# Four edits to an attention, experts and dense-layer kernel: where list scatters and weight loads stand, the mask's number type, and which engines decode w_out

## The chip, the core and the metric

The kernel runs on one core of a Trainium2 chip. A core has a matrix engine (TensorE, PE in the rows, with a separate weight load, PEld), a vector engine (VectorE, DVE), a scalar engine (ScalarE, ACT), a general engine (GpSimd, POOL) and SyncE (SP), which here only starts DMA transfers. The metric is the device time of one execution in microseconds (us), lower is better.

## The reference

Three stages follow one another, cut here to what is computed. The inputs are float32; the dense layer's two matrices arrive as float64.

```python
# attention: q, k, v are (4, 8, 576, 64)
scores = q @ k.T / 8
scores = where(block_of_64(i) >= block_of_64(j), scores, -1e9)
x = softmax(scores) @ v                 # then (2304, 512)
# routed experts: 8 of them, 512 -> 1024 -> 512
do = x @ w_skip > 0
e = argmax(x @ w_gate); gate = softmax(x @ w_gate)[e]
x[do] += gate * (relu(x @ w1[e]) @ w2[e])
# dense layer: 512 -> 2048 -> 512
h = x @ w_in
out = (max(h, 0) + alpha * min(h, 0)) @ w_out
```

## The kernel before

**Attention.** Two heads make a pair, and there are 16 pairs. A hand-written table of times (`OFF`) puts the steps of all pairs in one order. For each pair `sc` makes five tiles of scores. A score is a sum of three matmul groups over a high and a low float32r part of the query and key (`PARTS`); the two heads lie in the two halves of the array's rows. The first four tiles of a pair end with a matmul of `top` by `neg`, in bfloat16, that adds a large negative number to the masked 64 columns (L238). The fifth tile has all 576 columns and no mask (L242).

**Routing.** After each batch (four pairs) the tokens of each expert are ranked. GpSimd scatters each token's number and gate into lists in DRAM (`lst`, L495 in `send`). The rows of x lie in DRAM too (`xd`). For the first 32 rows of each expert there is a shortcut: GpSimd gathers these rows directly (`xgs`), TensorE transposes them, and ScalarE copies the result to `xts` (L687 and L688, in `trans`, called by `s_x`). All other rows are reached through the lists, which SyncE loads back (`load_list`).

**Experts.** `s_one(e)` and `s_two(e)` are the two matmul groups of expert e's first 32 rows. `extra(e)` handles further rows in chunks of up to 128 and is skipped by a branch when there are none; `level0(e)` gathers its first chunk ahead. Expert e+3's weights are loaded during expert e (`load_w`, w1 then w2, 4 pieces of 512 KB each). All large loads stand in one chain in which a load waits for the second-last before it (`DEPTH = 2`, in `bulk`), so two are in flight. `DEC[e]` says how many pieces of w_in or w_out are decoded during expert e before and after that load. A decode turns pairs of integers (a float64) into a float32, and then splits it into a high and a low part; each one also issues the load three pieces on, into one of three raw buffers (`dr`). From `last_exp` on the order is written by hand: routing, experts, then the dense layer.

**Dense layer.** Five windows of 512 rows (the last has 256). For every f of 16, `g1` is the first matmul group, `act` the slope and the split into `gh` (ScalarE) and `gl`, and `g2` the second group. `g1` runs two f ahead of `g2`, `act` one ahead. In the first window (w = 0, called window 0 here) the loop also decodes w_out, f+3 at step f (`w_dec`, with a part on ScalarE and GpSimd: L637, L648, L649) and splits it (`w_split`, L629 for the low part). At odd f it transposes 128 rows of the next window (`tr_x`) and splits them into `xs` (`split_x`, L853 on ScalarE and L854 on VectorE). The first two pieces of w_out are decoded during expert 5 by VectorE alone, into a tile called `xz`; the first window's rows also go to `xz` (L887), are transposed there (L896) and the last experts' results are added by TensorE (L899, which reads a selection matrix that VectorE makes at L882).

## Time and profile before

| | us |
|---|---|
| median of 3 runs | 865.99 (864.88 to 866.8) |
| the profiled execution, its own time | 870.16 |
| the profiled execution, its span | 868.6 |
| TensorE busy in the span | 800.6 (92%) |
| VectorE busy | 459.9 (53%) |
| ScalarE busy | 304.4 (35%) |
| GpSimd busy | 193.7 (22%) |

The profiled execution is one run and took 4.17 us more than the median of the runs. By the rows the span has five stages: attention to about 250 us, the routing tail to 288, the experts to about 406, the last expert with the hand-over to about 443, window 0 to about 542, and the other four windows to the end.

### The profile page before, as it was taken

The page shows a single profiled execution, that of the slowest core. Times are in us where ns is not written, and L with a number is a line of the kernel's source. Part 1 is how long each engine was busy: PE and PEld are TensorE (multiplying, and loading weights), DVE is VectorE, ACT ScalarE, POOL GpSimd, SP SyncE. Part 2 cuts the span into 40 slices and gives each one's busy share as a digit, 9 for nine tenths or more (in the row PEclk, how much of TensorE's full clock was granted, in tenths as well). Part 3 has the DMA queues.
Part 4 walks back from the last instruction along what each step waited for, and adds up shares of the span by engine and source line. Part 5 has one row for each costly group of instructions (what it writes and reads, how often), then busy time and mean ns, then how long its engine had stood idle before and what let it go on. Part 6 is the DMA issues. An engine that isn't in the chain of part 4 may idle for free.

```text
span 868.6 us, 14592 instructions
## 1 busy us (share of the span) xinstructions
PE 800.6 (92%) x5548; PEld 612.0 (70%) x5548; DVE 459.9 (53%) x931; ACT 304.4 (35%) x793; POOL 193.7 (22%) x225
## 2 busy tenths in 40 slices
PE   7999999999985999895499996999999999999998
PEld 4777777777742666663388675888888888888887
DVE  3466758576645397789359998222322222222232
ACT  3667676776631223112143354211121112111121
POOL 1000110100113014223025654222222221222132
PEclk7899999999986999999689999999999999999999
DMA  6674354455315787774632222100020001000000
GB/s 126 149 205 130 93 147 108 116 134 132 88 45 145 241 250 244 248 259 140 213 134 84 74 72 74 48 1 1 1 97 0 1 2 62 11 1 1 25 25 25
DMA packets 96376, 85.80 MB, mean 99 GB/s; under 512 B 68601, under 2 KB 73913, under 8 KB 96272
## 3 DMA queue, kind: packets, MB, share of 16 engines
q1 hardware_dynamic: 93776, 78.88, 31.2%
q0 software_dynamic: 2496, 5.61, 2.1%
q8 instruction: 57, 0.93, 0.4%
q14 instruction: 47, 0.39, 0.1%
HBM read 73.20 MB, written 11.71 MB: 98 GB/s over the span
## 4 chain that ended last, share of the span: by engine, by line
PE 56%; DVE 16%; DMA 15%; issue 5%; ACT 4%; SPq 1%; POOL 1%; another core or an unknown queue 1%; DVEq 0%; ACTq 0%; POOLq 0%
PE psf L966 18%; PE psa L998 6%; PE psa L999 6%; PE psa L1008 6%; DMA w1t<-in_moe_w_dram 5%; DMA w2t<-in_moe_w_dram 5%; PE pso L325 4%; PE pspt L300 4%; PE pss L236 3%; DMA dr<-in_moe_w_in_dram 3%; PE pss L242 2%; PE pso L313 2%; DVE mx L249 2%; DVE dt L638 2%; ACT pt L274 2%
## 5 line engine op out<-in xcount | busy, mean ns | idle before, releaser
L966 PE MATMUL psf<-xs,whi 128*128 128x512 f32 (+1 forms) x640 | 160.7, 373 | 6.1 <-ACT xs L853 6.1
L984 POOL TENSOR_TENSOR gl<-gt,gh 128x512 fp32r<-128x512 f32 (+1 forms) x72 | 85.4, 1186 | 250.5 <-PE psa L1008 136.0
L966 PEld LDWEIGHTS psf<-xs,whi 128*128 128x128 f32 x640 | 115.0, 189 | 31.4 <-ACT xs L853 6.7
L983 ACT ACTIVATE gh<-gt 128x512 fp32r<-128x512 f32 (+1 forms) x80 | 47.1, 588 | 255.7 <-PE psa L999 148.6
L979 DVE TENSOR_SCALAR gu<-psf,alf 128x512 f32<-128x512 f32 (+1 forms) x64 | 43.7, 682 | 165.6 <-PE psf L966 165.3
L966 PE MATMUL psf<-xs,wlo 128*128 128x512 f32 (+1 forms) x320 | 80.9, 375 | 0.0
L266 ACT ACTIVATE pe<-pss,mx 128x512 f32<-128x512 f32 (+3 forms) x128 | 66.6, 525 | 14.5 <-DVE mx L249 12.9
L966 PEld LDWEIGHTS psf<-xs,wlo 128*128 128x128 f32 x320 | 57.2, 189 | 12.0
L274 ACT ACTIVATE pt<-pspt 128x512 f32<-128x512 f32 (+3 forms) x112 | 51.9, 488 | 32.4 <-PE pspt L300 29.6
L998 PE MATMUL psa<-whi,gh 128*128 128x512 f32 x144 | 57.5, 400 | 4.0 <-ACT gh L983 4.0
L249 DVE TENSOR_REDUCE mx<-pss 128x2 f32<-128x1024 f32 (+1 forms) x64 | 52.3, 817 | 14.5 <-PE pss L238 10.5
L998 PE MATMUL psa<-wkg,gh 128*128 128x512 f32 x144 | 56.9, 395 | 2.0 <-ACT gh L983 2.0
L999 PE MATMUL psa<-wlo,gh 128*128 128x512 f32 x144 | 56.3, 391 | 0.0
L999 PE MATMUL psa<-wkg,gh 128*128 128x512 f32 x144 | 56.2, 390 | 0.0
L300 PE MATMUL pspt<-ident,pe 128*128 128x128 f32 x320 | 52.6, 292 | 0.1
L325 PE MATMUL pso<-pt,vr 128*64 128x256 f32 (+1 forms) x384 | 47.1, 356 | 3.6 <-ACT pt L274 3.6
L980 DVE SCALAR_TENSOR_TENSOR gt<-psf,gu 128x512 f32<-128x512 f32 (+1 forms) x64 | 40.0, 625 | 12.3 <-POOL gl L984 6.2
L703 PE MATMUL psh<-w1t,xts 128*32 128x256 f32 x256 | 22.3, 496 | 25.6 <-DMA w1t<-in_moe_w_dram 13.7
L854 DVE TENSOR_TENSOR xs<-psx,xs 128x512 fp32r<-128x512 f32 x18 | 12.4, 689 | 58.1 <-ACT xs L853 58.1
L325 PEld LDWEIGHTS pso<-pt,vr 128*64 128x64 f32 x384 | 29.9, 138 | 17.8 <-ACT pt L274 7.8
L638 DVE TENSOR_SCALAR dt<-dr 128x512 int32<-128x512 int32 x29 | 24.3, 838 | 32.0 <-DMA dr<-in_moe_w_in_dram 27.7
L300 PEld LDWEIGHTS pspt<-ident,pe 128*128 128x128 f32 x320 | 34.6, 144 | 7.1 <-issue 2.2
(237 smaller groups left out, 1455.7 us busy)
## 6 DMA issues: line engine op xcount, KB each, us to landing
w1t<-in_moe_w_dram SPq DMA_DIRECT2D x32, 512.0 KB
w2t<-in_moe_w_dram SPq DMA_DIRECT2D x32, 512.0 KB
dr<-in_moe_w_in_dram SPq DMA_DIRECT2D x16, 512.0 KB
dr<-in_moe_w_out_dram SPq DMA_DIRECT2D x16, 512.0 KB
out_dram<-ob SPq DMA_DIRECT2D x18, 256.0 KB
qr<-in_q_dram SPq DMA_DIRECT2D x32, 128.0 KB
kr<-in_k_dram SPq DMA_DIRECT2D x32, 128.0 KB
vr<-in_v_dram SPq DMA_DIRECT2D x32, 128.0 KB
```

Source lines behind the costliest of these rows:

```text
L249: nc.vector.tensor_reduce(out=m, in_=ps[:, :, 0:128 * i + 128], axis=AX.X, op=ALU.max, negate=True)
L266: ins = nc.scalar.activation(out=pt[:, x, 0:n], in_=ps[:, x, 0:n], func=AF.Exp, bias=m[:, x:x + 1], scale=1.0, accum_out=d["sum"][:, x * 4 ...
L274: nc.scalar.activation(out=o, in_=a, func=AF.Copy)
L300: nc.tensor.transpose(ps[:, y, j, :], e[:, x, j * 128:j * 128 + 128], ident)
L325: nc.tensor.matmul(d["o"][hs, c0:c0 + n * 128], v5[:, j, x, :], pt[:, x, 2 * j:2 * j + n].rearrange("p n c -> p (n c)"), start=(j == 0), s ...
L966: nc.tensor.matmul(ps[:, 0:n], wsp[f // 4 * 4 + kk][a][:, ws], c[:, kk, 0:n], start=(n0 == 0 and kk == 0), stop=(n0 == 2 and kk == 3))
L979: nc.vector.tensor_scalar(out=u[:, 0:n], in0=ps[:, 0:n], scalar1=0.0, scalar2=alf[:, f:f + 1], op0=ALU.min, op1=ALU.mult)
L983: nc.scalar.activation(out=hi[:, 0:n], in_=t[:, 0:n], func=AF.Copy)
L984: (nc.gpsimd if w or f % 2 else nc.vector).tensor_tensor(out=lo[:, 0:n], in0=t[:, 0:n], in1=hi[:, 0:n].bitcast(F32), op=ALU.subtract)
L998: nc.tensor.matmul(o, hi[:, ts], whi, start=(f == 0), stop=False)
L999: nc.tensor.matmul(o, hi[:, ts], wlo, start=False, stop=False)
L1008: nc.tensor.matmul(acc[w, t], lo[:, t * 128:t * 128 + 128], whi, start=False, stop=False)
```

## The change

It has four parts, which the diff shows in the order of the code.

1. The mask's two small operands become float32r, and the mask's matmul stands after the first of the three groups instead of behind the last.
2. The last batch's list scatters are no longer issued in `route5`. They are issued after `s_x(0)`, and the first of them waits for the ScalarE copy of the first rows. Four of the register loads of counts (`load_areg`) stand ahead of it. `s_one` of experts 1 and 2 stand right behind `s_one(0)`.
3. `DEC[4]` becomes (0, 3): during expert 4 the three decodes, with the loads of w_out that they issue, stand behind the load of expert 7's weights.
4. In window 0 the decode of w_out runs on VectorE alone. The negative part is scaled by a second ScalarE operation, the sum is one VectorE operation from PSUM as in the other windows, all `gl` are on GpSimd, and the next window's transposes stand two f earlier, with their split ahead of the decode.

```diff
--- before.py
+++ after.py
@@ -31,7 +31,7 @@
 PADROW = NT
 KX = 4
 DEPTH = 2
-DEC = ((0, 1), (2, 1), (2, 2), (2, 3), (3, 0), (0, 0), (0, 0), (0, 0))
+DEC = ((0, 1), (2, 1), (2, 2), (2, 3), (0, 3), (0, 0), (0, 0), (0, 0))
 ON_ACT = ("0", "1", "2a", "2b", "3a", "3b", "5", "xt")
 PSPLIT = (2, 3)
 EARLY = 2
@@ -144,12 +144,12 @@
     nc.vector.memset(fill, PADROW)
     tlo = acst.tile([128, 5], I32, name="tlo")
     nc.vector.tensor_scalar(out=tlo, in0=tok, scalar1=63, scalar2=None, op0=ALU.bitwise_and)
-    top = acst.tile([128, 128], BF16, name="top")
-    nc.vector.memset(top, 0.0)
+    top = acst.tile([128, 128], F32R, name="top")
+    nc.vector.memset(top.bitcast(F32), 0.0)
     for r in (0, 64):
-        nc.vector.memset(top[r:r + 1, 0:64], 1.0)
-    neg = acst.tile([128, 64], BF16, name="neg")
-    nc.vector.memset(neg, NEG)
+        nc.vector.memset(top[r:r + 1, 0:64].bitcast(F32), 1.0)
+    neg = acst.tile([128, 64], F32R, name="neg")
+    nc.vector.memset(neg.bitcast(F32), NEG)
     thi = acst.tile([128, 5], F32, name="thi")
     nc.vector.tensor_tensor(out=thi, in0=tok, in1=tlo, op=ALU.subtract)
     sli = const.tile([128, 2, 2], F32, name="sli")
@@ -233,9 +233,10 @@
             qc = slice(i * 128, i * 128 + 128)
             for k, (a, b) in enumerate(PARTS):
                 for x, hs in enumerate(half):
-                    nc.tensor.matmul(ps[:, x, 0:n], d[a][hs, qc], d[b][hs, 0:n], start=(k == 0), stop=False)
-            for x, hs in enumerate(half):
-                nc.tensor.matmul(ps[:, x, n - 64:n], top[hs], neg[hs], start=False, stop=True)
+                    nc.tensor.matmul(ps[:, x, 0:n], d[a][hs, qc], d[b][hs, 0:n], start=(k == 0), stop=(k == 2))
+                if k == 0:
+                    for x, hs in enumerate(half):
+                        nc.tensor.matmul(ps[:, x, n - 64:n], top[hs], neg[hs], start=False, stop=False)
         else:
             for c, o in ((slice(0, 512), ps[:, 0]), (slice(512, S), ps[:, 1, 0:64])):
                 for k, (a, b) in enumerate(PARTS):
@@ -490,16 +491,14 @@
         nc.vector.tensor_tensor(out=pi, in0=po, in1=nb, op=ALU.add)
         def send(ts=range(5)):
             for t in ts:
-                if b == B - 1:
+                if t and b == B - 1:
                     apart()
                 ins = nc.gpsimd.indirect_dma_start(out=lst, out_offset=bass.IndirectOffsetOnAxis(ap=pi[:, t, :], axis=0), in_=pr[:, t, :], in_offset=None, bounds_check=LROWS - 1, oob_is_err=False)
                 free(ins, "lst")
-                if b < B - 1:
+                if b < B - 1 or t == 0:
                     tc.add_manual_dep(ins.ins, last_exp[0].name, mybir.DependencyInfo(mybir.DependencyClass.Sync, mybir.DependencyReason.DATA), reason="list scatters apart")
 
         sends[b] = send
-        if b == B - 1:
-            send()
         tg = T5("tg", 3, BF16)
         nc.vector.tensor_copy(out=tg[:, :, 0:1], in_=gate)
         for i in (1, 2):
@@ -665,6 +664,7 @@
                 dec_load(m + 3)
 
     lv = lst.rearrange("(e r) c -> e r c", e=E)
+    AHEAD = 3
     li = [mw.tile([128, E, 2], I32, tag=f"li{i}", name="li", bufs=1) for i in range(KX)]
 
     def load_list(i):
@@ -685,7 +685,7 @@
             ps = ps_t.tile([128, 2, n], F32, tag="t", name="pst", padded_shape=[128, 4, 128])
             for i in range(2):
                 nc.tensor.transpose(ps[:, i], src[0:n, (j + i) * 128:(j + i) * 128 + 128], ident[0:n, 0:n])
-            nc.scalar.activation(out=o[:, j:j + 2, 0:n], in_=ps, func=AF.Copy)
+            last_exp[0] = nc.scalar.activation(out=o[:, j:j + 2, 0:n], in_=ps, func=AF.Copy).ins
 
     sx, sy, sh = {}, {}, {}
 
@@ -701,7 +701,7 @@
         for kk in range(4):
             for c in range(4):
                 nc.tensor.matmul(ps[c * 32:c * 32 + 32, :], sx[g][:, kk, r * 32:r * 32 + 32], wt[e][0][:, kk, c * 256:c * 256 + 256], start=(kk == 0), stop=(kk == 3), tile_position=(0, c * 32))
-        sh[e] = mw.tile([128, 256], F32, tag="sh", name="sh", bufs=1)
+        sh[e] = mw.tile([128, 256], F32, tag="sh", name="sh", bufs=AHEAD)
         nc.scalar.activation(out=sh[e], in_=ps, func=AF.Relu)
 
     def s_ht(e):
@@ -821,6 +821,9 @@
         with many.Else():
             ch.half()
 
+    load_areg(4)
+    s_x(0)
+    sends[B - 1]()
     for i in range(KX):
         load_list(i)
     load_w(2, range(4, 8))
@@ -833,11 +836,11 @@
 
     level0(0)
     level0(1)
-    load_areg(4)
-    s_x(0)
-    tc.mark_branch_hint_location("x0", "LikelyTaken", [ET.PE])
     s_one(0, load_areg)
     load_areg(2)
+    tc.mark_branch_hint_location("x0", "LikelyTaken", [ET.PE])
+    for e in range(1, AHEAD):
+        s_one(e)
     s_ht(0)
     xs = {}
     wkg = []
@@ -862,7 +865,7 @@
             hi, lo = (wk.tile([128, 512], F32R, tag=t, name="w" + t) for t in ("hi", "lo"))
         else:
             return
-        splits[f] = decode(16 + f, hi, lo, tmp, early, False)
+        splits[f] = decode(16 + f, hi, lo, tmp, True, False)
         if not early and f + 3 < 16:
             dec_load(16 + f + 3)
 
@@ -909,7 +912,8 @@
             level0(e + 2)
         if e + 1 < E:
             tc.mark_branch_hint_location(f"x{e + 1}", "LikelyTaken", [ET.PE])
-            s_one(e + 1)
+            if e + 1 >= AHEAD:
+                s_one(e + 1)
         if e + 1 == E:
             first_window()
         else:
@@ -973,15 +977,14 @@
         t = gp.tile([128, 512], F32, tag="gt", name="gt", bufs=1)
         if w == 0:
             nc.scalar.activation(out=u[:, 0:n], in_=ps[:, 0:n], func=AF.Relu, scale=-1.0)
-            nc.scalar.activation(out=t[:, 0:n], in_=ps[:, 0:n], func=AF.Relu)
-            nc.vector.scalar_tensor_tensor(out=t[:, 0:n], in0=u[:, 0:n], scalar=nalf[:, f:f + 1], in1=t[:, 0:n], op0=ALU.mult, op1=ALU.add)
+            nc.scalar.activation(out=u[:, 0:n], in_=u[:, 0:n], func=AF.Copy, scale=nalf[:, f:f + 1])
         else:
             nc.vector.tensor_scalar(out=u[:, 0:n], in0=ps[:, 0:n], scalar1=0.0, scalar2=alf[:, f:f + 1], op0=ALU.min, op1=ALU.mult)
-            nc.vector.scalar_tensor_tensor(out=t[:, 0:n], in0=ps[:, 0:n], scalar=0.0, in1=u[:, 0:n], op0=ALU.max, op1=ALU.add)
+        nc.vector.scalar_tensor_tensor(out=t[:, 0:n], in0=ps[:, 0:n], scalar=0.0, in1=u[:, 0:n], op0=ALU.max, op1=ALU.add)
         hi = gp.tile([128, 512], F32R, tag="gh", name="gh")
         lo = gp.tile([128, 512], F32R, tag="gl", name="gl")
         nc.scalar.activation(out=hi[:, 0:n], in_=t[:, 0:n], func=AF.Copy)
-        (nc.gpsimd if w or f % 2 else nc.vector).tensor_tensor(out=lo[:, 0:n], in0=t[:, 0:n], in1=hi[:, 0:n].bitcast(F32), op=ALU.subtract)
+        nc.gpsimd.tensor_tensor(out=lo[:, 0:n], in0=t[:, 0:n], in1=hi[:, 0:n].bitcast(F32), op=ALU.subtract)
         gt[w, f] = hi, lo
 
     acc = {}
@@ -1018,18 +1021,18 @@
     for n, (w, f) in enumerate(seq):
         if n + 2 < len(seq):
             g1(*seq[n + 2])
-        t = (f - 7) // 2
+        t = (f - 5) // 2
         px = None
         if w + 1 < len(wins) and f % 2 and 0 <= t < wins[w + 1][1] // 128:
             px = tr_x(w + 1, t)
         if n + 1 < len(seq):
             act(*seq[n + 1])
+        if px is not None:
+            split_x(w + 1, t, px)
         if w == 0:
             w_dec(f + 3, dt)
             if f:
                 w_split(f + 2)
-        if px is not None:
-            split_x(w + 1, t, px)
         if f == 13 and w + 2 < len(wins):
             load_x(w + 2)
         g2(w, f)
```

On SyncE, at expert 4, the large loads stood in this order before (`dr` are raw pieces of the dense layer's matrices, `w1t` and `w2t` expert 7's weights):

```order
L794 UNCONDITIONAL_BRANCH
L79 DMA dr<-in_moe_w_out_dram 128x1024 x3
L79 DMA w1t<-in_moe_w_dram 128x1024 x4
L79 DMA w2t<-in_moe_w_dram 128x2x512 x4
L794 COMPARE_AND_BRANCH
```

And now:

```order
L794 UNCONDITIONAL_BRANCH
L79 DMA w1t<-in_moe_w_dram 128x1024 x4
L79 DMA w2t<-in_moe_w_dram 128x2x512 x4
L79 DMA dr<-in_moe_w_out_dram 128x1024 x3
L794 COMPARE_AND_BRANCH
```

The three loads of w_out moved behind the eight of expert 7. The loads of the first window's rows (L887) stand behind all of them in both.

On VectorE, in the middle of window 0, one f with its decode read like this before (`dt` and `dr` are the decode's tiles, `gt` the sum of `act`):

```order
L977 SCALAR_TENSOR_TENSOR gt<-gu,nalf,gt 128x512
L984 TENSOR_TENSOR gl<-gt,gh 128x512
L638 TENSOR_SCALAR dt<-dr 128x512
L639 TENSOR_SCALAR dr<-dr 128x512
L640 TENSOR_SCALAR dt<-dt 128x512
L641 TENSOR_SCALAR dt<-dt 128x512
L642 SCALAR_TENSOR_TENSOR dt<-dt,dr 128x512
L643 TENSOR_SCALAR dr<-dt 128x512
L629 TENSOR_TENSOR wkg<-dt,wkg 128x512
L977 SCALAR_TENSOR_TENSOR gt<-gu,nalf,gt 128x512
```

And now (the lines are those of the changed kernel):

```order
L983 SCALAR_TENSOR_TENSOR gt<-psf,gu 128x512
L637 TENSOR_SCALAR dt<-dr 128x512
L638 TENSOR_SCALAR dr<-dr 128x512
L639 TENSOR_SCALAR dt<-dt 128x512
L640 TENSOR_SCALAR dt<-dt 128x512
L641 SCALAR_TENSOR_TENSOR dt<-dt,dr 128x512
L642 TENSOR_SCALAR dr<-dt 128x512
L644 SCALAR_TENSOR_TENSOR dr<-dr 128x512
L645 TENSOR_TENSOR dt<-dt,dr 128x512
L628 TENSOR_TENSOR wlo<-dt,whi 128x512
L983 SCALAR_TENSOR_TENSOR gt<-psf,gu 128x512
L857 TENSOR_TENSOR xs<-psx,xs 128x4x128
```

Two operations of the decode came from GpSimd to VectorE (L644, L645), `gl` left VectorE in every second f, and `gt` now reads PSUM (`psf`). Where there is an `xs`, it follows `gt` directly.

On GpSimd, at the routing tail, the gathers of the first rows (`xgs`) and the list scatters stood so before:

```order
L590 DMA xgs<-xd,sid 128x512
L65 MEMSET pad 1x1
L590 DMA xgs<-xd,sid 128x512
L65 MEMSET pad 1x1
L495 DMA lst<-pr,pi 19456x2
```

And now:

```order
L589 DMA xgs<-xd,sid 128x512
L65 MEMSET pad 1x1
L589 DMA xgs<-xd,sid 128x512
L679 TENSOR_LOAD cnt x4
L496 DMA lst<-pr,pi 19456x2
```

Four register loads came between, and the first scatter waits for ScalarE. Four more scatters follow in both, and then the gathers through the lists.

## Rows read from the trace of the kernel before

**Rows 1.** Busy time (instructions) by stage, then granted TensorE clock, DMA share, GB/s.

```profile
0.00:250.00 250.00, 238.24 (x2188) 174.38 (x2188) 154.02 (x439) 166.78 (x517) 21.61 (x71) 0.96 0.51 125
...
443.00:542.00 99.00, 88.11 (x377) 68.64 (x378) 88.80 (x128) 43.92 (x80) 52.20 (x35) 0.98 0.25 80
542.00:868.60 326.60, 321.96 (x1504) 265.95 (x1503) 91.02 (x140) 54.58 (x95) 74.95 (x65) 0.99 0.06 20
```

**Rows 2.** End of the experts, TensorE: start, us, line, work, idle before.

```profile
392.71 3.19 PE L785 MATMUL psy<-w2t,hT 128*64 128x256 f32 x28
...
414.37 1.08 PE L703 MATMUL psh<-w1t,xts 128*32 128x256 f32 x8 [9.07 <-DMA w1t<-in_moe_w_dram]
...
437.60 2.59 PE L899 MATMUL psx<-xz,ys 128*128 128x128 f32 x13
```

**Rows 3.** The same stretch, SyncE: its DMA issues.

```profile
394.42 14.14 SPq L79 DMA_DIRECT2D dr<-in_moe_w_out_dram  x3
```

**Rows 4.** The chain of waits there: start, us, what.

```profile
412.93 4.37 DMA w1t<-in_moe_w_dram
417.32 4.92 DMA w1t<-in_moe_w_dram
...
431.67 4.06 DMA xz<-xd
```

**Rows 5.** End of a score tile: TensorE (PE) and weight loads (PEld).

```profile
174.41 0.19 PEld L242 LDWEIGHTS pss<-kl,qd 128*128 128x128 f32 x1
...
174.52 0.19 PEld L242 LDWEIGHTS pss<-kh,qd 128*128 128x128 f32 x1
...
175.82 0.10 PEld L238 LDWEIGHTS <-top 64*128 64x128 bf16 x2 [0.28 <-issue]
...
175.96 0.42 PEld L201 LDWEIGHTS psq<-ident,qr 128*128 128x128 f32 x4
```

**Rows 6.** Routing tail, all engines.

```profile
259.03 1.04 POOL L495 DMA_INDIRECT lst<-pr,pi  x1 [0.22 <-DVE tg L508]
...
261.28 0.63 PE L687 MATMUL pst<-ident,xgs 128*128 128x128 f32 x4 [1.64 <-issue]
...
266.51 0.66 ACT L688 ACTIVATE xts<-pst 128x256 f32<-128x256 f32 x2 [13.71 <-remote]
...
279.25 0.95 POOL L590 DMA_INDIRECT xg<-xd,li  x1 [0.73 <-POOL pad L65]
...
288.32 0.38 PE L687 MATMUL pst<-ident,xg 128*128 128x128 f32 x2
```

**Rows 7.** VectorE decoding a piece of w_out (after the last of w_in).

```profile
410.04 0.43 DVE L639 TENSOR_SCALAR dr<-dr 128x512 int32<-128x512 int32 x1
...
413.82 0.42 DVE L638 TENSOR_SCALAR xz<-dr 128x512 int32<-128x512 int32 x1
...
418.06 0.87 DVE L882 TENSOR_SCALAR xz<-iot,sidf 128x128 f32<-128x128 bf16 x4
```

**Rows 8.** Window 0, all engines.

```profile
452.60 0.75 DVE L977 SCALAR_TENSOR_TENSOR gt<-gu,nalf,gt 128x512 f32<-128x512 f32 x1 [0.28 <-ACT gt L976]
...
457.02 0.74 DVE L977 SCALAR_TENSOR_TENSOR gt<-gu,nalf,gt 128x512 f32<-128x512 f32 x1
...
503.44 0.68 DVE L629 TENSOR_TENSOR wlo<-dt,whi 128x512 fp32r<-128x512 f32 x1
...
506.68 1.50 POOL L984 TENSOR_TENSOR gl<-gt,gh 128x512 fp32r<-128x512 f32 x1
...
507.05 1.42 DVE L639 TENSOR_SCALAR dr<-dr 128x512 int32<-128x512 int32 x1
...
531.53 0.93 DVE L977 SCALAR_TENSOR_TENSOR gt<-gu,nalf,gt 128x512 f32<-128x512 f32 x1
...
541.08 0.58 ACT L853 ACTIVATE xs<-psx 128x512 fp32r<-128x512 f32 x1
...
541.71 2.08 PE L966 MATMUL psf<-xs,whi 128*128 128x512 f32 x4 [5.41 <-ACT xs L853]
```

## The prediction

> **What bounds the kernel now.** I read the table of stages first, because the share of the whole span (TensorE 92%) hides where time is lost. In attention TensorE is busy 238.24 of 250 us and in windows 1 to 4 321.96 of 326.6 [rows 1]: there only TensorE's own work counts. Window 0 is different: VectorE is busy 88.8 of 99 us and TensorE 88.11 [rows 1]. The timeline of the last expert shows the other loss: TensorE stands 9.07 us at 414.37 for expert 7's w1, and the hand-over matmuls start only at 437.60 [rows 2]. SyncE's row says why the weights are late: it sat 14.14 us, from 394.42 to 408.56, in the issue of three w_out pieces [rows 3], which wait for raw buffers that VectorE's decode frees; expert 7's weights are queued behind. From 408 on the chain of waits is one transfer after another [rows 4]. So the kernel can win at the hand-over and in window 0, and lose in attention. The profiled execution took 870.16 us, 4.17 more than the median 865.99; I sum against its own time and carry the difference over to the median.
>
> **Part 3, expert 7's weights first.** Before, their first transfer could not start before 408.56 [rows 3]. Now it needs SyncE, free at 394.42 [rows 3], and the buffer of expert 4's w1. The last full chunk of expert 4 is in its second matmul group, which reads w2, from 392.71 to 395.90 [rows 2], so w1's buffer is free by then: I take 395.5. Eight pieces follow, two in flight, and a step of the chain takes 4.37 to 4.92 us [rows 4]; four pairs at 4.4 end at 413. The first two w_out pieces land a step later, 417.5; the third and the first window's rows are issued at about 418, and the rows, at the 4.06 us of the chain [rows 4] and some queueing, are there at 424. TensorE's transposes of them take about 4 us. VectorE decodes the two w_out pieces from 417.5 at 4.24 us each (413.82 to 418.06) and makes the selection matrix in 0.87 [rows 7]: 426.9. Both paths end near 427.5 to 428, against 437.60: **−10**. TensorE's own work on experts 6 and 7 still lies beside the transfers. What is late next is VectorE's decode, now behind the w_out pieces; before, its last operation began at 418.06 [rows 7], 19 us ahead of its use. Bounds: −6 if every step takes 4.92 and the rows come a step later; −15 if the rows don't queue and TensorE alone is left.
>
> **Part 4, window 0.** The loop's pace is that of `gt`: from 457.02 to 531.53, 11 steps of f take 74.5 us, 6.77 each [rows 8]. VectorE is held up in them by GpSimd: a decode operation that takes 0.43 alone [rows 7] takes 1.42 when `gl` runs [rows 8], so one `gl` costs 0.99. Now a step of VectorE is `gt` 0.74 [rows 8], a whole decode 4.24 [rows 7], the low part 0.68 [rows 8], and one hold-up by `gl`, 0.99: 6.65. In four of the eleven steps `xs` follows `gt` and waits for `gh` and its own high part on ScalarE, two operations of about 0.58 (541.08 [rows 8]) and the signals between, about 1.4 in all, and takes 0.68 as the low part does; the `gl` runs meanwhile and holds nothing up: 1.4 + 0.68 − 0.99 = +1.1 each. Eleven steps: 73.2 + 4.4 = 77.6, or +3.1. The step before them had 4.42 (452.60 to 457.02 [rows 8]) and gets 6.65: +2.2. Against this, the wait of 5.41 us of TensorE at 541.71 for `xs` [rows 8] goes away, since the last split now stands at f = 11, where no decode is ahead of it; and the matmuls behind it ran slow, 2.08 for four [rows 8] against a mean of 0.86 (321.96 us for 1504 [rows 1]), so that about 1 more comes back. I give 6.3 back in all. Sum: **−1**. On ScalarE one operation replaces another and L637 goes; GpSimd loses its part of each decode and gains a `gl` in every second f: both have less to do than VectorE in a step, and lie beside it. The unknown is the hold-up. With none, VectorE needs 5.66 and TensorE's pace decides, 5.75 (321.96 us for three and a half windows of 16 steps [rows 1]): 11 × −1.02 + 4.4 + 1.3 − 6.3 = −12. With two operations held up, 1.98, it is 12 × 0.99 more: +11. I take one, because the row shows one operation held for the length of one `gl`.
> Of this port the Trainium skill ("SBUF — State Buffer", Who interferes with whom) says that VectorE and GpSimd share a pair of ports which whoever issues first holds for the whole instruction, with the other fully blocked, and that a VectorE instruction with at most one SBUF input outside the fast modes isn't touched. The trace agrees: 1.42 instead of 0.43. By the rule alone the price is up to a whole `gl`.
>
> **Part 1, the mask.** Attention is TensorE's, so 64 mask pairs (16 pairs of heads, 4 tiles) each count. At the end of a tile the mask costs 0.14 (its load at 175.82, the next group's at 175.96), and its load takes 0.10; a float32r load takes 0.19, but 64-column float32r matmuls follow each other at 0.11 (174.41 to 174.52), with the load hidden [rows 5]. For one mask pair (two half-height loads) that gives 0.11 if the halves load side by side and 0.22 if not: −0.03 to +0.08 a tile, −2 to +5 over 64. I take **+2**, between, since no row shows two float32r loads of half height before so short matmuls.
> Against this edit speaks a rule of the Trainium skill ("TensorE: Matmul & The Clock Gate", Weight-path perf modes): a fast weight load is on for 128 weights of a type other than FP32. The rows agree, 0.10 against 0.19. If all of the 0.09 were exposed, the sum would have +6 here in place of +2; the 0.11 between short float32r matmuls says that it is hidden.
>
> **Part 2, the routing tail.** The first rows' transposes are at 261.28 and end by 261.9, but ScalarE copies them only at 266.51, when the five scatters (the first at 259.03) have been issued [rows 6]; the row names no engine that it waited for. If the scatters hold it up, the copy now comes at 262 and the scatters from 262.5: lists and all behind them 3.5 later. The four register loads on GpSimd lie in the wait. The gather at 279.25 [rows 6], two behind the lists, then is at about 282.8, and its rows land at 287, with the 4.06 of the chain's transfer of rows [rows 4]. What follows on TensorE, expert 2's first chunk at 288.32 [rows 6], no longer waits for `s_one(2)`, which stood just before it and is now done ahead, but for these rows: 287.3, **−1**. If the copy was late for another reason and stays at 266.51, the scatters start 7.5 to 8 late, and the chunk 4 to 5: bounds −4 and +5. Behind it on GpSimd are only the gathers that this counts; SyncE's w2 load of expert 2 is as late as the lists, and needed last.
>
> **Sum.** −10 − 1 + 2 − 1 = −10: 860 for the profiled execution, **856** for the median. Windows 1 to 4 have the same operations and are at TensorE's pace. A difference under 0.2% (1.7 us) can't be told from none.
>
> **Rivals.**
> *VectorE and GpSimd collide twice per step (slower).* The place is the loop of window 0, where `gl` is now on GpSimd in every f, and VectorE's nine operations are back to back. The forecast flips when a step is 0.83 above 6.65, at 7.5 us (10 / 12); with two operations held up, 7.64, the sum is +2: 868. For it: `gl` itself took 1.50 under this traffic [rows 8], and VectorE was busy nine tenths of that stage [rows 1]. Against: GpSimd's decode operations, which held up VectorE as well, are gone.
> *The port costs a whole `gl`.* 1.50 in place of 0.99, 12 times: +6, so 862. For it is the rule above; against it the one row.
> *No hold-up at all.* Part 4 gives −12: 845. For it: half of the VectorE operations are not the fast 0.43 kind, and `gt` reads PSUM.
> *The scatters' wait costs 4 to 5* (the copy isn't held up by the scatters): 861.
> *Expert 7's weights come early, but the hand-over then waits for w_out's decode.* If the w_out pieces come a step or so later than I think, to 422, the selection matrix is ready at 431.4 and part 3 gives only −6: 860. For it: the decode of both pieces is in front of that operation on VectorE.
> *Parts 2 and 3 both fall short and window 0 is a little slow:* 866, no change.
>
> **Chances and range.** The forecast, 852 to 861 by its own bounds, 0.40; no hold-up 0.12; a whole `gl` 0.08; the wait for the copy 0.10; the decode 0.10; several short, 0.08; collision 0.12. The range is 843 to 867: it takes in all but the collision and the edges of the rest. Faster: the first five, 0.80. Same 0.08, slower 0.12.
>
> **What would show it.** Part 3: SyncE issues w1 of expert 7 near 395, TensorE's wait of 9 us is shorter and earlier, the hand-over matmul (L899 before) starts near 428. Part 4: `gt` to `gt` 6.6 us, 7.7 with an `xs`; no wait at the first group of window 1; one decode operation of about 1.4 per `gl`. Part 1: the attention ends within 250 and 254 us, and the next group's load comes directly behind the last score group. Part 2: the copy at about 262, the lists' scatters behind, expert 2's chunk at 287. I am wrong if the copy stays at 266, if steps in window 0 are over 7.5, or if L899 is still behind 433.

## The result and the profile after

The changed kernel takes 855.7 us in the median of 10 runs (853.08 to 858.76), against 865.86 of 10 runs before; the ratio is 0.9902 (95% interval 0.9878 to 0.9926), so 8.5 us faster. One run of the kernel before took 983.9 us and isn't in the ratio. Beside other kernels, later, the ratio was 0.9922 (0.9897 to 0.9948). The forecast was 856. The two first profiles are 16.1 us apart (spans 868.6 and 852.5), but 5.9 of that is chance: the execution profiled before took 4.3 us more than its median and that of after 1.6 less. So I compare stretch by stretch, each from its own first event.

The table of stages after, with cuts at its own places. The columns are those of [rows 1]: the stretch and its length; busy time of TensorE, its weight loads, VectorE, ScalarE and GpSimd; granted TensorE clock, DMA share, GB/s.

```profile
0.00:250.00 250.00, 241.14 (x2196) 175.06 (x2197) 155.44 (x446) 167.48 (x518) 21.57 (x71) 0.97 0.51 125
...
432.00:532.00 100.00, 91.79 (x395) 72.27 (x396) 89.31 (x148) 39.31 (x68) 21.05 (x15) 1.00 0.24 79
532.00:852.50 320.50, 316.20 (x1487) 261.37 (x1485) 90.65 (x140) 53.92 (x94) 74.95 (x65) 1.00 0.06 20
```

From window 1's first output to the end it is 224.6 us against 225.0 before, and attention is 2 us longer (table below). Window 0 is still full of VectorE work. The difference is at the borders. First the hand-over, on TensorE (answers to [rows 2]):

```profile
389.17 3.67 PE L785 MATMUL psy<-w2t,hT 128*64 128x256 f32 x32
...
408.98 2.74 PE L703 MATMUL psh<-w1t,xts 128*32 128x256 f32 x19 [3.96 <-PEq L794]
...
422.74 4.01 PE L899 MATMUL psx<-ident,xz 128*128 128x128 f32 x16 [3.70 <-DMA xz<-xd]
426.54 4.96 PE L902 MATMUL psx<-xz,ys 128*128 128x128 f32 x32
```

The wait of 9.07 us for expert 7's w1 is gone. The 3.96 that stand there now are put down to TensorE's own sequencer at a branch (`PEq L794`), not to w1. The hand-over matmul starts at 426.54. That is 33.7 us behind the end of expert 4's last chunk (389.17 + 3.67 = 392.84), where it was 41.7 behind it (395.90). VectorE has the selection matrix for it ready at 424.70:

```profile
423.84 0.86 DVE L885 TENSOR_SCALAR xz<-iot,sidf 128x128 f32<-128x128 bf16 x4
```

SyncE shows why the hand-over is earlier (answers to [rows 3]):

```profile
391.15 6.60 SPq L79 DMA_DIRECT2D w1t<-in_moe_w_dram  x4
399.45 8.18 SPq L79 DMA_DIRECT2D w2t<-in_moe_w_dram  x4
410.33 5.32 SPq L79 DMA_DIRECT2D dr<-in_moe_w_out_dram  x3
419.89 1.75 SPq L890 DMA_DIRECT2D xz<-xd  x4
```

w1 is issued at 391.15, ahead of w_out, without the 14 us. The chain of waits there (answers to [rows 4]) is still one transfer after another, but with a piece in it that I had not put into my sum:

```profile
389.19 1.95 PE psy L785 x16
391.15 3.61 DMA w1t<-in_moe_w_dram
394.78 4.61 DMA w1t<-in_moe_w_dram
...
410.33 4.93 DMA dr<-in_moe_w_out_dram
...
416.32 3.29 issue
...
419.89 2.71 DMA xz<-xd
```

w1 follows expert 4's second matmul group (L785), and no decode. The 3.29 us of issue at 416.32 lie on SyncE between the branch around expert 7's further rows and the loads of the first window's rows (L890); what SyncE waits for isn't in the profile. The chain before has the same piece:

```profile
426.84 3.57 issue
```

In window 0, all engines (answers to [rows 8]; L640 is the decode operation that stands where `gl` runs, L857 the split):

```profile
466.89 0.68 DVE L983 SCALAR_TENSOR_TENSOR gt<-psf,gu 128x512 f32<-128x512 f32 x1
467.49 0.42 DVE L637 TENSOR_SCALAR dt<-dr 128x512 int32<-128x512 int32 x1
...
468.38 1.49 POOL L987 TENSOR_TENSOR gl<-gt,gh 128x512 fp32r<-128x512 f32 x1 [4.94 <-ACT gh L986]
...
468.74 1.41 DVE L640 TENSOR_SCALAR dt<-dt 128x512 int32<-128x512 int32 x1
...
473.31 0.69 DVE L983 SCALAR_TENSOR_TENSOR gt<-psf,gu 128x512 f32<-128x512 f32 x1
...
474.80 1.31 POOL L987 TENSOR_TENSOR gl<-gt,gh 128x512 fp32r<-128x512 f32 x1 [4.93 <-ACT gh L986]
...
475.24 0.69 DVE L857 TENSOR_TENSOR xs<-psx,xs 128x512 fp32r<-128x512 f32 x1 [1.24 <-ACT xs L856]
...
480.80 0.68 DVE L983 SCALAR_TENSOR_TENSOR gt<-psf,gu 128x512 f32<-128x512 f32 x1
...
523.95 0.50 PE L1001 MATMUL psa<-whi,gh 128*128 128x512 f32 x1 [1.67 <-ACT gh L986]
...
526.81 1.09 PE L970 MATMUL psf<-xs,whi 128*128 128x512 f32 x4
```

A step from `gt` to `gt` takes 6.42 us (466.89 to 473.31), or 7.49 with a split of the next window (to 480.80). One VectorE operation takes 1.41 when GpSimd's `gl` starts, and the split waits 1.24 for ScalarE. At the end TensorE goes into window 1's first group without a wait (526.81); its longest stop near there is 1.67. The granted clock shows what else the old wait cost. The first of these two rows is of before, behind the 5.41 us in which TensorE stood; the second is of the changed kernel:

```profile
541.70:545.00 3.30, 3.29 (x8) 2.62 (x9) 1.54 (x3) 1.56 (x3) 0.79 (x1) 0.50 0.00 0
526.00:531.00 5.00, 4.40 (x20) 3.27 (x19) 3.62 (x7) 1.32 (x3) 0.61 (x1) 1.00 0.00 0
```

Before, window 1's first groups ran at a granted clock of 0.50, the lower of the two levels (1.2 GHz): four matmuls took 2.08 us [rows 8]. Now they run at 1.00 (2.4 GHz), and four take 1.09.

At the routing tail (answers to [rows 6]) ScalarE's copy follows its transposes at once, and the scatters follow the copy:

```profile
258.27 0.95 PE L687 MATMUL pst<-ident,xgs 128*128 128x128 f32 x4 [1.65 <-issue]
258.83 0.81 ACT L688 ACTIVATE xts<-pst 128x256 f32<-128x256 f32 x2 [7.73 <-PE pst L687]
...
259.92 1.01 POOL L496 DMA_INDIRECT lst<-pr,pi  x1 [4.21 <-ACT xts L688]
...
280.81 0.94 POOL L589 DMA_INDIRECT xg<-xd,li  x1 [0.73 <-POOL pad L65]
280.86 3.21 PE L719 MATMUL psy<-w2t,hts 128*32 128x128 f32 x56 [4.47 <-issue]
...
284.94 1.46 PE L687 MATMUL pst<-ident,xg 128*128 128x128 f32 x4 [0.25 <-DMA xg<-xd,li]
```

The end of a mask in attention (answers to [rows 5]): its load and the load of the second score group.

```profile
176.32 0.19 PEld L239 LDWEIGHTS pss<-neg,top 64*128 64x128 f32 x2
...
176.49 0.19 PEld L236 LDWEIGHTS pss<-kl,qh 64*128 64x128 f32 x2
```

### The profile page after: what moved, and what is told of

Its sections match the earlier page's. It is cut to its first block, busy times and chain, and to the rows that moved or that the text cites. A ratio compares the mean times of both kernels' runs of the same rounds, so it can differ in the third digit from the quotient of the medians.

```text
span 852.5 us, 14562 instructions
## 1 busy us (share of the span) xinstructions
PE 799.0 (94%) x5548; PEld 613.9 (72%) x5548; DVE 458.8 (54%) x951; ACT 299.3 (35%) x779; POOL 162.4 (19%) x204
## 4 chain that ended last, share of the span: by engine, by line
PE 47%; DVE 9%; DMA 4%; issue 2%; ACT 1%; SPq 0%; DVEq 0%; ACTq 0%
PE psf L970 18%; PE psa L1001 6%; PE psa L1002 6%; PE psa L1011 6%; PE psh L752 4%; PE psy L763 3%; DVE dt L640 2%; DMA w2t<-in_moe_w_dram 1%; DVE dr L644 1%; DVE dt L641 1%; DVE gt L983 1%; DMA w1t<-in_moe_w_dram 1%; PE psh L777 1%; DVE dr L642 1%; DVE dr L638 1%
## 5 line engine op out<-in xcount | busy, mean ns | idle before, releaser
L987 POOL TENSOR_TENSOR gl<-gt,gh 128x512 fp32r<-128x512 f32 (+1 forms) x80 | 96.0, 1200 | 322.9 <-ACT gh L986 190.5
L275 ACT ACTIVATE pt<-pspt 128x512 f32<-128x512 f32 (+3 forms) x112 | 52.1, 488 | 29.4 <-PE pspt L301 28.7
L983 DVE SCALAR_TENSOR_TENSOR gt<-psf,gu 128x512 f32<-128x512 f32 (+1 forms) x80 | 51.0, 637 | 13.9 <-POOL gl L987 8.1
L857 DVE TENSOR_TENSOR xs<-psx,xs 128x512 fp32r<-128x512 f32 x18 | 12.4, 692 | 60.4 <-ACT xs L856 60.4
L326 PEld LDWEIGHTS pso<-pt,vr 128*64 128x64 f32 x384 | 30.1, 136 | 16.9 <-ACT pt L275 7.2
L752 PEld LDWEIGHTS psh<-xT,w1t 128*128 128x128 f32 x320 | 39.5, 205 | 1.5 <-issue 1.0
L752 PE MATMUL psh<-xT,w1t 128*128 128x128 f32 x320 | 40.2, 290 | 0.0
```

Source lines behind the costliest of these rows:

```text
L275: nc.scalar.activation(out=o, in_=a, func=AF.Copy)
L326: nc.tensor.matmul(d["o"][hs, c0:c0 + n * 128], v5[:, j, x, :], pt[:, x, 2 * j:2 * j + n].rearrange("p n c -> p (n c)"), start=(j == 0), s ...
L752: nc.tensor.matmul(ps[:, f], w[:, kk, c:c + 128], self.xT[:, kk], start=(kk == 0), stop=(kk == 3))
L983: nc.vector.scalar_tensor_tensor(out=t[:, 0:n], in0=ps[:, 0:n], scalar=0.0, in1=u[:, 0:n], op0=ALU.max, op1=ALU.add)
L987: nc.gpsimd.tensor_tensor(out=lo[:, 0:n], in0=t[:, 0:n], in1=hi[:, 0:n].bitcast(F32), op=ALU.subtract)
```

## The experiments

"Before" and "changed" are the two kernels. All ratios are to the kernel before, measured beside it. One table has the stretches of all profiles, in us, worked out as differences of starts in the timelines: attention from the first to the last pair's copy of its output; from the first gather of first rows to the gather of expert 2's first chunk (G), to the end of expert 4's last chunk (X), to the hand-over matmul (H); and in the dense layer from the first group to the `gt` of f = 2 (S), from there to that of f = 13 (L), from there to window 1's first output (E).

| kernel | attention | G | X | H | S | L | E |
|---|---|---|---|---|---|---|---|
| before | 211.2 | 22.8 | 139.4 | 181.1 | 14.0 | 74.5 | 112.1 |
| changed | 213.2 | 27.3 | 139.4 | 173.1 | 15.4 | 74.9 | 105.3 |
| changed, again | 213.3 | 26.4 | 144.5 | 180.7 | 15.5 | 74.8 | 105.3 |
| mask alone | 213.2 | 23.3 | 143.1 | 181.9 | 14.0 | 74.5 | 113.1 |
| tail alone | 211.3 | 26.9 | 141.3 | 185.2 | 14.3 | 74.5 | 111.9 |
| tail, w2 first | 211.3 | 26.5 | 143.8 | 179.3 | 14.3 | 74.5 | 113.2 |
| weights alone | 211.3 | 22.6 | 139.8 | 175.0 | 14.0 | 74.5 | 112.3 |
| window alone | 211.2 | 24.4 | 138.6 | 183.9 | 15.1 | 74.9 | 105.4 |
| changed without tail | 213.3 | 23.2 | 134.4 | 174.8 | 15.1 | 74.9 | 105.3 |
| gl on VectorE | 213.4 | 27.7 | 138.2 | 176.0 | 15.1 | 76.4 | 107.4 |
| split late | 213.3 | 28.5 | 143.4 | 176.8 | 15.5 | 73.0 | 105.3 |
| both | 213.3 | 27.7 | 140.4 | 175.5 | 15.1 | 70.3 | 107.4 |
| shift undone | 213.2 | 27.6 | 144.8 | 180.3 | 15.5 | 73.8 | 111.4 |
| best | 211.2 | 22.6 | 138.9 | 177.1 | 15.1 | 72.9 | 105.3 |

Attention, S, L and E repeat within 0.4 us wherever their code is the same, but for E, which spreads over 1.3 in the kernels with the old window. X and H spread over 4 to 8 us between profiles of like kernels, so single differences there say little.

**Part 1 alone.**

```diff
...
+        if k == 0:
+            nc.tensor.matmul(ps[:, x, n - 64:n], top[hs], neg[hs], start=False, stop=False)
...
```

> The kernel before with part 1 alone (the mask in float32r behind the first group). My theory, from the two profiles: from the first pair's last copy of attention output to the last pair's, 213.2 us after against 211.2 before, so 0.13 us a pair; the whole kernel gets 2 us slower, ratio 1.002 (1.001 to 1.004). Rival: the mask costs nothing because its float32r weight load is hidden behind the first group, and the 2 us came from another edit or from chance: ratio 1.000 and 211.2 us between the two copies.

Measured: 1.0017 (0.999 to 1.0045), no clear difference by the clock of the whole. Attention is 213.2 against 211.2: the theory holds for the stretch. All eight profiles with the float32r mask have 213.2 to 213.4, the six without it 211.2 or 211.3. The type and the place of the mask change together here, so which of the two costs the 2 us isn't shown.

**Part 2 alone.**

```diff
...
-        if b == B - 1:
-            send()
...
+    load_areg(4)
+    s_x(0)
+    sends[B - 1]()
...
```

> The kernel before with part 2 alone (last list scatters behind the copy of the first rows, three s_one ahead). My theory: the copy comes right behind its transposes instead of 4.6 us later, the lists come 2 to 3.5 us later, and from the first gather of rows to the first chunk of expert 2 there are 31.5 us in place of 31.84; the whole is within 1 us of before, ratio 0.999 to 1.001. Rival: the routing tail, which was 3.4 us shorter after the change, is shorter because of this part: ratio about 0.996.

Measured: 1.0047 (1.0021 to 1.0074), about 4 us slower; neither theory. Its timeline of the tail:

```profile
256.22 0.66 ACT L687 ACTIVATE xts<-pst 128x256 f32<-128x256 f32 x2 [7.59 <-PE pst L686]
...
257.15 1.01 POOL L495 DMA_INDIRECT lst<-pr,pi  x1 [3.92 <-ACT xts L687]
...
277.90 0.94 POOL L588 DMA_INDIRECT xg<-xd,li  x1 [0.73 <-PEq L793]
...
283.59 0.09 POOL L65 MEMSET pad<- 1x1 f32 x1 [4.74 <-DMA xg<-xd,li]
...
286.07 7.60 PE L751 MATMUL psh<-xT,w1t 128*128 128x128 f32 x64
```

The copy is early, the first scatter 6.15 us behind the first gather (at 251.00; 2.55 before), and the gather for expert 2, 26.9 behind it, lands only at 283.59, 5.7 us after its issue.

**Part 3 alone.**

```diff
-DEC = ((0, 1), (2, 1), (2, 2), (2, 3), (3, 0), ...
+DEC = ((0, 1), (2, 1), (2, 2), (2, 3), (0, 3), ...
```

> The kernel before with part 3 alone (expert 7's weights ahead of the three w_out loads). My theory: SyncE issues expert 7's w1 near 392 to 395 in place of 408.6, the hand-over matmul starts 8 us (7 to 10) earlier relative to the end of expert 4's last chunk, and the whole kernel gains as much: ratio 0.991 (0.988 to 0.993). Rival: window 0 is limited by VectorE, whose decode now starts later (415 in place of 409.6), and gives half of it back: ratio 0.995 to 0.996.

Measured: 0.992 (0.9888 to 0.9952), 6.9 us; H is 175.0 against 181.1, and behind the end of expert 4's last chunk (H less X) the hand-over comes 6.5 us earlier, a little less than the 7 to 10 expected. The weights go ahead on SyncE:

```profile
392.73 6.54 SPq L79 DMA_DIRECT2D w1t<-in_moe_w_dram  x4
401.32 8.38 SPq L79 DMA_DIRECT2D w2t<-in_moe_w_dram  x4
411.93 4.95 SPq L79 DMA_DIRECT2D dr<-in_moe_w_out_dram  x3
```

S, L and E are as before: nothing is given back in window 0, though VectorE's decode of w_out starts 22.2 us behind the end of expert 4's last chunk, 13.7 before. The rival falls.

**Part 4 alone.**

```diff
-        splits[f] = decode(16 + f, hi, lo, tmp, early, False)
+        splits[f] = decode(16 + f, hi, lo, tmp, True, False)
...
-        t = (f - 7) // 2
+        t = (f - 5) // 2
```

> The kernel before with part 4 alone (window 0). My theory: steps of 6.4 us, 7.5 where next-window rows are split, so no gain in the loop (0 to +2 us), and 6 to 7 us gained at the hand-over to window 1, where TensorE no longer waits 5.4 us for the last split: about -5 us, ratio 0.994 (0.992 to 0.997). Rival: this part alone gains nothing, since the end of window 0 is set by VectorE's total of decodes either way: ratio 1.000.

Measured: 0.9935 (0.9906 to 0.9963), 5.6 us. The stretches agree: S 1.1 longer, L 0.3 longer, E 6.7 shorter, 5.3 in all.

**The changed kernel without part 2.**

```diff
...
+        if b == B - 1:
+            send()
...
-    load_areg(4)
-    s_x(0)
-    sends[B - 1]()
...
```

> The changed kernel without part 2 (the routing tail as before). Part 2 alone had cost 0.47% of the time, where I forecast -1 us. My theory: the lists come 3.5 us later, and with them the chain of large loads up to expert 7's weights; in the kernel before, these weights ended the wait at the hand-over, so all of it counted; with part 3 they wait for expert 4's buffers instead, so most of it is covered, and taking part 2 out of the changed kernel changes little: ratio 0.989 to 0.991 against before. Rival: the 4 us are lost ahead of expert 2's first chunk, whatever follows; then this kernel has 0.985 to 0.987.

Measured: 0.9864 (0.9817 to 0.9911). That is the rival's value, but its interval takes in my theory's. X is 134.4, and 134.4 to 139.8 in the three kernels with part 3 and without part 2, against 138.2 to 144.8 in the six with both (means 137.7 and 141.8). So part 2 probably costs in the changed kernel too, though little of it is left at the hand-over: H has 175.6 and 177.1 in the mean of the same kernels. This profile holds a surprise:

```profile
257.56 1.04 POOL L496 DMA_INDIRECT lst<-pr,pi  x1 [0.21 <-DVE tg L509]
...
259.78 0.63 PE L688 MATMUL pst<-ident,xgs 128*128 128x128 f32 x4 [1.60 <-issue]
...
260.22 0.66 ACT L689 ACTIVATE xts<-pst 128x256 f32<-128x256 f32 x2 [8.95 <-PE pst L688]
...
278.16 0.95 POOL L591 DMA_INDIRECT xg<-xd,li  x1 [0.71 <-POOL pad L65]
```

The scatters start as before (257.56), and yet the copy comes 0.4 behind its transposes.

**`gl` on VectorE, behind the decode.**

```diff
-        nc.gpsimd.tensor_tensor(out=lo[:, 0:n], ...
+        def low():
+            (nc.gpsimd if w else nc.vector).tensor_tensor(out=lo[:, 0:n], ...
...
                 w_split(f + 2)
+            while lows:
+                lows.pop(0)()
...
```

> The changed kernel with gl of window 0 on VectorE, behind the decode's low part, for f of 1 to 13. My theory (GpSimd's gl holds up one VectorE operation by 0.97 us a step): no decode operation takes 1.4 us any more, a step is 0.60 + 4.25 + 0.60 + 0.60 = 6.05 us in place of 6.42, and 8.1 in place of 7.48 where the next window is split, since there the gl was hidden; over eleven steps 74.7 against 74.9, so no difference in the whole: ratio 0.989 to 0.992 against before. Rival: the long operation is not held up by GpSimd (it waits for something of its own) and stays at 1.4: then steps are 7.0 and the kernel is 6 to 7 us slower, ratio 0.997.

Measured: 0.9917 (0.9886 to 0.9948), no clear difference from the changed kernel (0.9902, and 0.9922 later). VectorE's groups in the loop (count, then busy us and mean ns), the decode operation of 1.41 among them, with GpSimd idle:

```profile
L989 DVE TENSOR_TENSOR gl<-gt,gh 128x512 fp32r<-128x512 f32 x10 | 6.9, 686 | 0.0
L640 DVE TENSOR_SCALAR dt<-dt 128x512 int32<-128x512 int32 x9 | 3.8, 428 | 0.3
```

And in the changed kernel:

```profile
L640 DVE TENSOR_SCALAR dt<-dt 128x512 int32<-128x512 int32 x10 | 10.1, 1012 | 0.3
```

428 ns against a mean of 1012: GpSimd's `gl` is what holds it up. Steps are 6.24, 0.2 more than the sum (between the `gl` and the next `gt` 0.2 go that I don't explain), and 8.18 with a split. By the stretches this kernel is not equal to the changed one: S, L and E together are 198.9 against 195.6.

**The split behind the decode.**

```diff
-        if px is not None:
-            split_x(w + 1, t, px)
         if w == 0:
             w_dec(f + 3, dt)
             if f:
                 w_split(f + 2)
+        if px is not None:
+            split_x(w + 1, t, px)
```

> The changed kernel with the next window's split again behind the decode (the transposes stay two f earlier). My theory: the gain at the hand-over to window 1 comes from the two f, not from the place ahead of the decode; the four steps with a split take 6.42 + 0.6 = 7.0 to 7.1 in place of 7.48, and there is no wait at the first group of window 1: 1.5 us faster than the changed kernel, ratio 0.987 to 0.990 against before. Rival: the split behind the decode comes late at f = 11 and TensorE waits for it again: 3 to 5 us slower than the changed kernel.

Measured: 0.9874 (0.9829 to 0.9919). Steps with a split take 7.02 in place of 7.49, L is 1.9 shorter, E the same 105.3. The two f earlier are enough at f = 11.

**Both.**

```diff
...
+            while lows:
+                lows.pop(0)()
+        if px is not None:
+            split_x(w + 1, t, px)
```

> The changed kernel with both: gl of window 0 on VectorE and the next window's split behind it. My theory: steps of 6.05 us, and 6.65 with a split, so eleven steps take 69 us in place of 74.9 and the kernel is 5 to 6 us faster than the changed one: ratio 0.983 to 0.985 against before. Rival: TensorE, with transposes and waits for the late gl, can't follow at 6.05 and sets steps of about 6.5: gain 2 us or less.

Measured: 0.9871 (0.9829 to 0.9913). Steps are 6.24 and 6.65 and L 70.3 (the theory had 6.05, 6.65 and 69), but E is 2.1 longer, and the sum of S, L and E (192.8) is 1.0 shorter than with the split late (193.7). TensorE's only waits from 515 to 545 us:

```profile
518.88 1.20 PE L1017 MATMUL psa<-whi,gl 128*128 128x512 f32 x4 [0.44 <-DVE gl L989]
...
525.53 1.21 PE L1017 MATMUL psa<-whi,gl 128*128 128x512 f32 x4 [0.80 <-DVE gl L989]
```

With 1.24 us of wait in 30, TensorE itself is the bound here, as the rival says. The rival's size was not right either: steps are not 6.5, and S, L and E together gain 2.8 on the changed kernel (195.6), between the rival's 2 or less and the theory's 5 to 6.

**Part 2 with expert 2's w2 ahead of the lists.** The kernel before with part 2 and:

```diff
+    load_w(2, range(4, 8))
     for i in range(KX):
         load_list(i)
-    load_w(2, range(4, 8))
```

> The kernel before with part 2, and SyncE issuing expert 2's w2 ahead of the list loads instead of behind them. Part 2 alone had cost 0.47%. My theory: it cost that because the list loads, and with them expert 2's w2 and every large load that is chained behind it, came 3.5 us later up to expert 7's weights. Then this order frees the chain from the lists: from the first gather to the issue of expert 7's w1 there are 152 to 153 us again in place of 155.7, and the ratio to before is 0.997 to 1.002. Rival: the time is lost in what waits for the lists themselves (the gathers, the branches), and stays: 1.003 to 1.006.

Measured: 0.9972 (0.9948 to 0.9995), 6.4 us faster than part 2 alone. The lists and their gathers are as late (G 26.5), but expert 7's w1 is issued 149.6 us behind the first gather in place of 155.7, and H is 5.9 shorter. In a kernel without part 3 the place of this load reaches the end through the chain of large loads. The run does more than undo a delay, though: w2 is issued from 2.9 us behind the first gather on, where it was 16.8 with part 2 alone and 12.7 before, and it gains 6.4 us where part 2 had cost 4.1. So it doesn't show that all of the 4.1 came this way.

**The transposes not shifted.**

```diff
-        t = (f - 5) // 2
+        t = (f - 7) // 2
```

> The changed kernel with the next window's transposes at the f of before (7, 9, 11, 13), the split still ahead of the decode. My theory: the last split, at f = 13, has no decode ahead of it, so it is done about 2 us after the gt of f = 14; TensorE waits there, but less than the 5.4 us of before: 2 to 3 us slower than the changed kernel, ratio 0.992 to 0.994 against before. Rival one: only the two f earlier matter, and the wait is 5 us again with slow matmuls behind it: 6 to 7 us slower, 0.997 or 0.998. Rival two: the place ahead of the decode is enough: same as the changed kernel.

Measured: 0.9963 (0.9932 to 0.9994), against 0.9922 of the changed kernel beside it: 3.5 us slower, though the two intervals overlap. Its profiled execution took 8 us more than its median, so I read only the border of the windows: E is 6.0 longer, L 1.0 shorter. TensorE at window 1's first group:

```profile
542.41 2.07 PE L970 MATMUL psf<-xs,whi 128*128 128x512 f32 x4 [3.87 <-ACT xs L856]
544.28 1.91 PE L970 MATMUL psf<-xs,wlo 128*128 128x512 f32 x4
```

It waits 3.87 and then runs slow, 1.91 for four, at a granted clock of 0.50:

```profile
542.40:544.30 1.90, 1.89 (x5) 1.50 (x6) 1.46 (x3) 1.68 (x3) 0.83 (x1) 0.50 0.00 0
```

This lies between my 2 to 3 and the first rival's 6 to 7; that the place alone is enough is wrong.

**Best.** The kernel before with part 3, and of part 4 all but the place of the split:

```diff
-DEC = ((0, 1), (2, 1), (2, 2), (2, 3), (3, 0), ...
+DEC = ((0, 1), (2, 1), (2, 2), (2, 3), (0, 3), ...
...
-        splits[f] = decode(16 + f, hi, lo, tmp, early, False)
+        splits[f] = decode(16 + f, hi, lo, tmp, True, False)
...
-        t = (f - 7) // 2
+        t = (f - 5) // 2
...
```

> The kernel before with part 3, the window's part 4 but the split behind the decode, and neither the mask's part 1 nor part 2. My theory: 2.0 us for the mask and 1.5 to 2 for the split less than the changed kernel, and nothing for part 2, which is covered there: 3.5 to 4 us faster than the changed kernel in the same call, ratio 0.985 (0.983 to 0.988) against before. Rival: the parts hide each other, and it is as fast as the changed kernel.

Measured: 849.09 us, 0.9807 (0.9776 to 0.9837): clearly faster than the kernel before and than the changed one (0.9922). The gain over the changed kernel beside it, 10.7 us in the medians, is more than expected: 2.1 in attention and 1.9 in L are what I expected; the rest lies between routing and hand-over (H 177.1 against 180.7 in those two profiles). Part 2 is there, but H differs as much between like kernels, so this run doesn't show that part 2 is the cause.

**The changed kernel again.**

> The changed kernel once more, beside the other kernels of this call. Theory: 0.990 against before (0.9878 to 0.9926 measured), with 0.13 us a pair more in attention, 7 to 8 us less at the hand-over and 5 less around window 0. Rival: the 16 us by which the two first profiles differ are the change, and the ratio is 0.982.

Measured: 859.76 us, 0.9922 (0.9897 to 0.9948). The rival falls: the 16 us of the first two profiles were not the change. Of the theory the ratio, attention and window 0 hold (S, L and E together are 5.0 shorter). The hand-over of this profile doesn't show the 7 to 8 us: H is 0.4 shorter than before, and H less X 5.5.

## Why the prediction was right, and where it was not

The time was met, but by terms that made up for each other: that it came out within 1 us is luck. For parts 1 to 4 I had forecast +2, −1, −10 and −1; alone they cost +1.5, +4.1, −6.9 and −5.6 us, together −6.9.

*Part 3, −10:* the mechanism is as told. SyncE no longer waits for VectorE's decode, the weights follow expert 4's last chunk, and the hand-over comes earlier: H is 173.1 to 180.7 in the nine profiles with part 3 (mean 176.6) and 179.3 to 185.2 in the five without it (mean 182.3). The size was too large, and the mis-sized term is the stretch from w1 to the first window's rows: I had them issued 22.5 us behind it (395.5 to 418); it was 28.7 (391.15 to 419.89). In it are the 3.29 us behind a branch, which stand in the chain of before as well, where I had summed transfers only; and the four steps of the chain took 19.2 (391.15 to 410.33) and not 17.5. Window 0 gave nothing back. The rival in which the hand-over waits for w_out's decode falls: the selection matrix was ready 1.8 us ahead (424.70, 426.54).

*Part 4, −1:* the steps were right in kind, and the experiments show each cause. One decode operation is held up by each `gl` (1.41, and 0.43 without GpSimd). With a split a step takes 1.07 more (I had 1.1). The border to window 1 gained 6.7 (I had 6.3), and it is the two f that give it; the slow matmuls in it are those at the granted clock of 0.50. The mis-sized term is the step: 6.42, not 6.65. I had used the durations of `gt` and the low part (0.74 and 0.68), but the next operation starts 0.60 behind each (466.89 to 467.49 for `gt`), so over eleven steps the loop lost 0.3 and not 3.1; and the start lost 1.4 where I had 2.2. The rival of two collisions falls with these steps, and that of none with the 1.41. For that last one my sum was wrong as well: without a hold-up there is none that a split could hide, so a split costs 5.66 + 1.4 + 0.68 − 5.75 = 2.0 and not 1.1. The sum should have read −8, and the rival 849.
The rival in which a `gl` costs its whole 1.50 falls: the hold-up is 0.98, and `gl` itself takes 1.49 where it starts beside a VectorE operation and 1.31 where VectorE stands idle. The trace agrees with the lock that the Trainium skill states ("SBUF — State Buffer", Who interferes with whom): the decode operation that starts behind `gl` (468.74, `gl` 468.38) waits, and the split, which has one input from PSUM and so only one from SBUF, isn't touched: it takes 0.69 while `gl` is under way (475.24, `gl` 474.80 to 476.11).

*Part 1, +2:* right, 2.0 in every profile, though I had only taken a value between −2 and +5. The mask's load and the next one are 0.17 apart (176.32 to 176.49) where the old one had 0.14 [rows 5]: 64 of these 0.03 make 2. Whole tiles agree: over the 40 in which the eight matmuls stand together, a tile takes 0.88 us to the next instruction with the new mask and 0.85 with the old. The fast weight load of the Trainium skill ("TensorE: Matmul & The Clock Gate", Weight-path perf modes) is on for 128 weights of types other than FP32. The trace agrees if float32r counts as FP32, since the load takes 0.19 in place of 0.10; but most of the difference is hidden.

*Part 2, −1:* this step failed. I had the lists 3.5 us late, which is what happened (the first scatter is 3.6 later behind the first gather), but then wrote that expert 2's w2, as late as the lists, is needed last, and that the first chunk would only wait for its rows. The w2-first run shows for the kernel without part 3 that this load is not one to leave for last: it stands ahead of the other large loads in their chain, and with it moved ahead expert 7's weights came 6.1 earlier. I also had the gathered rows land 4 us after their gather; they took 5.7 with part 2 alone and 4.1 in the changed kernel (280.81 to 284.94). And the gain on the other side, an earlier `s_one`, was worth little, since most of the second matmul group of expert 1, which stands ahead of expert 2's chunk, still runs only from 280.86 (L719, 56 of its 64 matmuls; the profile names nothing that they waited for).

One stretch shows the loss. From the first gather to expert 2's first transposes, where I had 1 us less, the eight profiles with part 2 have 31.5 to 36.3 us (mean 33.3) and the six without it 27.6 to 32.6 (mean 30.1). That the scatters hold up ScalarE's copy is only partly true: it was late in five of the six profiles with the old order and not in the sixth, and never with the new order.
What stays open is how much part 2 costs where part 3 is in. The changed kernel without it is faster by 0.4 to 0.6 points, but the intervals overlap, and of the 3 us at expert 2's first transposes H keeps 1.5 in the mean, within its spread.

## What to carry to other kernels

Ask of every transfer what it stands in front of, on its queue and in its chain: part 3 gained by taking three loads out from under expert 7's weights, and part 2 lost by making the lists late that stand ahead of another. Sum a loop from start to start, not from durations, and read the pace of the engine behind the bound as well: taking 4.6 us from VectorE's loop gave 2.8 before TensorE set the pace. When a total comes out as forecast, time the parts alone: here four terms were off by 0.5 to 5 us and cancelled.

## What the hardware showed that I had not expected

Profiles of one kernel differ by 5 to 8 us between the routing and the hand-over (H 173.1 and 180.7 for the changed kernel), and in the start of attention (its first output copy at 31.5 to 37.2 us), while the loops of window 0 repeat to 0.02 us. On SyncE, a stretch of 3.3 us follows a branch with nothing to wait for in the profile. A low-part operation on VectorE is followed by the next one 0.60 after its start, though it lasts 0.68.
